# Bucketed attention ahead of two feed-forward layers on one core: value products in pairs from the start, other shares of the PSUM banks, partial sums exchanged by ScalarE

## The chip, the cores and the metric

The kernel runs on one core of a Trainium2 chip. The metric is the device time of one execution in microseconds (us); lower is better. Engines are named as in the profile: PE is TensorE's matmul stream and PEld its weight loads, DVE is VectorE, ACT is ScalarE, POOL is GpSimd, SP is SyncE, whose queue issues every DMA here (SPq in the rows).

## The reference, cut to what matters

```python
B, H, S, D = q.shape                                  # 2, 8, 768, 64
q_bits = (np.einsum('bhsd,dk->bhsk', q, proj) > 0)    # 6 bits a token, k alike
mask = q_bucket[:, :, :, None] == k_bucket[:, :, None, :]
scores = scale * np.matmul(q, k.transpose(0, 1, 3, 2))
scores = np.where(mask, scores, -1000000000.0)
scores = scores - np.max(scores, axis=-1, keepdims=True)
attn = np.exp(scores)
attn = attn / (np.sum(attn, axis=-1, keepdims=True) + 1e-09)
x = np.matmul(attn, v)                                # then 1536 tokens x 512
h = x @ w_in
x = (h * np.tanh(softplus(h))) @ w_out                # 512 -> 2048 -> 512
# then gate logits, 8 rounds of row and column scaling, and 8 experts,
# each relu(x @ w1[e]) @ w2[e], added with their weights
```

Attention has 16 heads of 768 tokens. The first feed-forward layer and the eight experts follow it on the same core. The change lies in attention, which takes about the first sixth of the time.

## The kernel before, in words

Attention works on half heads: 32 units `u`, each 384 queries of one head against its 768 keys. The heads 0 and 1 come first with both their halves (`u` 0 and 1 are head 0, `u` 2 and 3 head 1); after that two neighbouring heads alternate. Two half heads of equal half from two neighbouring heads make a pair `n` (`members`): pair 0 is `u` 0 and 2, pair 1 is `u` 1 and 3, pair 2 is `u` 4 and 5, and so on, 16 pairs. For a half head:

- `s_mm` makes the masked scores with queries on the partitions, in three tiles of 128 queries, each in one of two double banks of the ring `ps_r`; `s_max` (DVE) takes their row maximum; `rows_mm` (PE, `prow`) turns the maxima into a row, `rows_cp` (DVE) limits it, and a DMA carries it to the operand of the next step.
- `st_mm` makes the scores again, transposed: six chunks of 128 keys by 384 queries, two matmuls each (lines 408 and 409), in the two banks of `ps_t`; `st_exp` (ACT) writes their exponentials into one of `NP` = 14 tiles `p`, each with two tiny extra columns.
- `add` (POOL) sums three chunks of `p` into a tile `pa`, in two additions; there are two such tiles for a half head.
- the value product multiplies three chunks of `p` with `v` into a tile `pav` of 64 partitions for a half head. For the pairs 0 and 1, `av_one` does it for one half head at a time; from pair 2 on `av_mm` does it for both members, and a chunk's two matmuls go to different halves of TensorE's columns. `pav` has two banks, one for even and one for odd pairs (`ps_a`).
- `sum_mm` (`psum`, ring `ps_r`) sums the `pa` of a pair over the partitions: each member leaves two partial sums, in two groups of 32 partitions.
- `norm` ends a pair in parts: 0 transposes the sums (DVE, `rs`), 1 copies one column of 32 to `own` (ACT), four small DMAs (`norm_move`) bring the neighbouring group's copy to `other`, 3 adds the two and takes the reciprocal (DVE, `nr`), 4 transposes it back (DVE), 5 multiplies `pav` with it (DVE, `xu`), 6 and 7 split the result into a rounded tile `xh` (ACT) and the rest `xl` (POOL or DVE). Only part 5 makes the bank of `pav` free.

Queries and keys of a head are loaded into a landing tile `raw` (one, `NRAW` = 1, besides special places for the heads 1 and 2), split into a rounded part and a rest (`prep_hi`, `prep_lo`), moved by DMAs to the operands (`prep_move`, `bits_move`), and multiplied with the projection for the bucket bits (`bits_mm`, `pbits`; `bits_cmp`). In gaps of the engines the first weights of the layer that follows are loaded and decoded (`decode`, eight parts; part 6 is POOL's, part 7 an addition on DVE or POOL) and converted (`weight_hi` on ACT, `weight_lo` on POOL).

The order of all this on each engine is not written out: a small planner in the kernel lists the tasks with costs (`COST`), predecessors and due times, shifted by a table `OFF`, and emits the next task of the engine that is free first. Where it expects TensorE to be idle early on, it puts short filler matmuls (`keep_warm`, line 295, which write `warm`). Behind attention the first layer begins (`up`, lines 789 to 791, tile `h`); its fourth weight tile is converted only behind the last part of `norm`, since its memory was attention's.

Of the kernel before, what the change touches and what calls it, by code (L numbers as in the profile page):

```python
# [16 lines left out]
P = 128  # L17
# [21 lines left out]
NRAW = 1  # L39
NP = 14  # L40
NPA = 6
AVG = 3
AVD = 6
ENTER = 0.14
LEAVE = 0.2
ADDS = "P"
# [4 lines left out]
OFF = {'weight_lo': 16.9, 'add': -3.4, 'weight_load': -20.3, 'norm6': 66.2, 'prep_hi': -4.2, 'norm_move': -19.9, 'load_qk': 0.9, 'norm0': -16.1, 'load_v': -23.6, 'decode': 9.4, 'bits_mm': -6.9, 'norm1': -61.2, 'norm5': 11.9, 'st_exp': -7.0, 'norm7': 23.6, 'rows_cp': -10.6, 'av_mm': 0.7, 'rows_move': -20.0, 'rows_mm': 3.0, 'norm4': -35.4, 'norm3': 9.3, 'sum_mm': -0.6, 'bits_cmp': -14.6, 'av_one': 3.6, 'weight_hi': 63.6, 's_max': 0.0, 'st_mm': 2.1, 'prep_move': 6.5, 'prep_lo': -0.4, 'bits_move': -5.8, 's_mm': 2.4}  # L51
DELTA = 0.0524
# [3 lines left out]
PACE = 24  # L56
# [15 lines left out]
def lsh_attention_moe_kernel(  # L72
# [111 lines left out]
    def attention():  # L184
        with ExitStack() as a:
# [23 lines left out]
            xu = out_p.tile([P, 2, 512], F32, name="xu")  # L209
            rs = out_p.tile([P, S], F32, name="rs")  # L210
            nr = out_p.tile([P, HALF // 32], F32, name="nr")
            own, other = (out_p.tile([P, HALF // 32], F32, name=n) for n in ("own", "other"))
# [17 lines left out]
            def pair_of(u):  # L230
                return u % 2 if u < 4 else u // 2

# [42 lines left out]
            def clear_slots(j):  # L275
                for y in ps[j::2]:
                    nc.gpsimd.memset(y[:, HALF:WIDE], TINY)
# [6 lines left out]
            def warm_up():  # L284
                warm.append(slot(ps_t, "t", 0, 2, [P, 512], F32, "warm"))
                for _ in range(WARM):
                    nc.tensor.matmul(warm[0], xh[:, 0, 0:P], xh[:, 0, 0:512], start=True, stop=True)

            def keep_warm(n):
                if nm(av_one, 0, 0) in ends:  # L290
                    return
                if nm(st_mm, 0, 0) in ends and len(warm) == 1:
                    warm.append(slot(ps_a, "a", 0, 2, [P, 512], F32, "warm"))
                for _ in range(n):
                    nc.tensor.matmul(warm[-1][:, :FILL], xh[:, 0, 0:P], xh[:, 0, 0:FILL], start=True, stop=True)
# [47 lines left out]
            def bits_mm(h):  # L343
                psb_t[h] = next_r("pbits")[:, 0] if h else slot(ps_a, "a", 1, 2, [P, 512], F32, "pbits")
# [85 lines left out]
            def av_chunks(n, us, g):  # L430
                if n not in av_t:
                    av_t[n] = slot(ps_a, "a", n, 2, [P, 512], F32, "pav")
                for c in range(AVG * g, AVG * g + AVG):
                    for u in us:
# [5 lines left out]

            def av_one(u, g):
                av_chunks(pair_of(u), (u,), g)

            def av_mm(n, g):
                av_chunks(n, members(n), g)
# [42 lines left out]
            def task(engines, due, f, *args, after=(), cost=None, lag=0.01, ring=None, frees=None):  # L488
# [4 lines left out]
                "E": dict(warm_up=2.6, bits_mm=0.36, s_mm=0.355, rows_mm=0.06, st_mm=0.355, av_mm=0.66 * AVG, sum_mm=0.67, av_one=0.66 * AVG),  # L493
# [9 lines left out]
                    clear=0.6, prep_lo=1.0, add=1.03, norm=1.0, decode=1.3, weight_lo=1.27,  # L503
# [13 lines left out]
            def av_done(u, g):  # L517
                return nm(av_one, u, g) if u < 4 else nm(av_mm, pair_of(u), g)
# [10 lines left out]
            for j in range(2):  # L529
                task("P", -20 + j, clear_slots, j, cost=0.35)  # L530
# [41 lines left out]
            for u in range(NU):  # L572
# [14 lines left out]
                for c in range(NKC):  # L587
                    i = 6 * u + c
                    old = order[i - NP] if i >= NP else None
                    task("E", i - 4.0, st_mm, u, c, after=ready + [nm(st_exp, *order[i - 2])] * (i > 1))  # L590
# [7 lines left out]
            for n in range(NU // 2):  # L598
# [3 lines left out]
                room = [nm(norm, n - 2, 5)] if n > 1 else [nm(bits_cmp, 0, 1, 0)] * n  # L602
                for g in range(NKC // AVG):
                    for part in [(u,) for u in us] if n < 2 else [us]:
                        f, x = (av_one, part[0]) if n < 2 else (av_mm, n)
                        task("E", 6 * part[-1] + AVG * g + AVD, f, x, g,
                             after=[nm(st_exp, u, c) for u in part for c in range(AVG * g, AVG * g + AVG)] + ([nm(f, x, g - 1)] if g else room)
                             + [nm(load_v, head(u)) for u in part] + [nm(clear_slots, j) for j in range(2)] * (n < 2))
# [7 lines left out]
                task("D", due, norm, n, 3, cost=0.35, after=[nm(norm_move, n, x) for x in range(4)] + [nm(norm, n - 1, 4)] * (n > 0))  # L616
# [16 lines left out]
            for n in range(NCH):  # L633
# [5 lines left out]
                for part, (e, cost) in enumerate(costs):  # L639
# [4 lines left out]
                        7: [nm(decode, i, j, 6)] + ([nm(weight_lo, i - NDEC, 1)] if i >= NDEC else []),  # L644
# [32 lines left out]
            def groups(k):  # L677
                return int(tasks[k][3] in (bits_mm, rows_mm, av_one, av_mm, sum_mm))

            def begin(e, k):  # L680
# [8 lines left out]
                if e == "E":  # L689
                    real += (0.0, ENTER, LEAVE)[groups(k) - mode[0]]  # L690
# [14 lines left out]
            while count < len(tasks):  # L705
# [13 lines left out]
                if e == "E":  # L719
                    mode[0] = groups(k)  # L720
# [46 lines left out]
    nc.vector.memset(csum, 0.0)  # L767
# [230 lines left out]
    at(NST - 9, open_t)  # L998

# [326 lines left out]
```

## Time and profile before

| | us |
|---|---|
| runs of the kernel before, median of 3 | 1507.12 |
| their lowest and highest | 1504.7 and 1508.23 |
| the profiled execution's own time | 1506.02 |
| the span of its profile | 1504.2 |

The span is the time between the first and the last recorded instruction; 1.8 us of the profiled execution's time lie around it. The granted clock of TensorE was 1.00 throughout. A matmul's row is longer than the time that it holds up the next one, since matmuls are pipelined: what a matmul costs is read from its start to the start of the next.

### The profile page before, as it was taken

What the parts mean: (1) busy time and instruction counts of PE and PEld (TensorE: products, weight loads), DVE (VectorE), ACT (ScalarE), POOL (GpSimd) and SP (SyncE); (2) the same over time, 40 slices, a digit from 0 to 9 for tenths busy, and PEclk for the clock granted to TensorE, in tenths of its full rate; (3) what the DMA queues carried; (4) which work ended last, traced back from release to release, by engine and by line L of the source; (5) the groups of instructions that cost most, each with busy time, mean ns of one, the idle gap of its engine ahead of it and who ended that gap; (6) DMA issues with size and microseconds to landing.
All of it is one profiled execution on the core that took longest, in us unless ns stands there. A gap on an engine that the chain in (4) does not pass through costs nothing.

```text
span 1504.2 us, 20253 instructions
## 1 busy us (share of the span) xinstructions
PE 1487.8 (99%) x7448; PEld 1254.2 (83%) x7448; DVE 866.2 (58%) x1394; ACT 628.9 (42%) x1113; POOL 910.8 (61%) x756
## 2 busy tenths in 40 slices
PE   9999999999999999999999999999999999999998
PEld 5555556888887899989899998989989899998987
DVE  6888886877625566665445467653534535344353
ACT  4555555544334343334334333343433334333331
POOL 7787874433222776666666666666666666666660
PEclk9999999999999999999999999999999999999999
DMA  7666531222200122222122222232222212222211
GB/s 181 168 153 165 155 82 43 87 80 72 70 1 15 45 83 70 71 70 71 58 69 70 71 70 71 64 106 70 70 71 70 65 64 69 70 71 71 71 43 42
DMA packets 69563, 116.81 MB, mean 78 GB/s; under 512 B 21348, under 2 KB 23512, under 8 KB 69464
## 3 DMA queue, kind: packets, MB, share of 16 engines
q1 hardware_dynamic: 69464, 115.53, 25.8%
q8 instruction: 58, 0.95, 0.3%
q14 instruction: 41, 0.34, 0.1%
HBM read 93.41 MB, written 3.15 MB: 64 GB/s over the span
## 4 chain that ended last, share of the span: by engine, by line
PE 93%; DVE 2%; DMA 2%; SPq 1%; issue 1%; ACT 0%; POOL 0%; DVEq 0%; ACTq 0%
PE y L1178 35%; PE u L1111 31%; PE y L814 9%; PE pav L436 4%; PE h L791 3%; PE h L790 3%; PE h L789 3%; PE pst L408 2%; PE ps L373 2%; PE pst L409 1%; DMA raw<-in_qk_dram 1%; DVE mx L378 1%; PE psum L452 1%; SPq L329 1%; PE pbits L347 0%
## 5 line engine op out<-in xcount | busy, mean ns | idle before, releaser
L1119 ACT ACTIVATE gh<-c 128x384 fp32r<-128x384 f32 x256 | 134.6, 526 | 174.3 <-DVE c L1131 172.3
L1131 DVE TENSOR_TENSOR u<-u,p 128x384 f32<-128x384 f32 x64 | 35.7, 558 | 283.7 <-PE u L1111 283.7
L1124 DVE SCALAR_TENSOR_TENSOR gl<-c,gh 128x384 fp32r<-128x384 f32 x256 | 196.0, 828 | 0.0
L1178 PE MATMUL y<-ww,gh 128*128 128x512 f32 x768 | 186.6, 391 | 0.0
L1178 PE MATMUL y<-w,gh 128*128 128x512 f32 x768 | 186.0, 391 | 0.0
L1178 PEld LDWEIGHTS y<-w,gh 128*128 128x128 f32 x768 | 143.7, 188 | 28.9
L1178 PEld LDWEIGHTS y<-ww,gh 128*128 128x128 f32 x768 | 143.7, 188 | 28.8
L994 POOL TENSOR_TENSOR w<-stage,w 128x1024 fp32r<-128x1024 f32 x32 | 76.3, 2386 | 89.1 <-ACT w L990 89.1
L994 POOL TENSOR_TENSOR ww<-stage,ww 128x1024 fp32r<-128x1024 f32 x32 | 76.3, 2384 | 81.7 <-ACT ww L990 81.7
L414 ACT ACTIVATE p<-pst 128x384 f32<-128x384 f32 x192 | 88.4, 490 | 79.1 <-PE pst L409 73.0
L814 PE MATMUL y<-gh,w 128*128 128x512 f32 x336 | 109.7, 389 | 0.0
L158 POOL TENSOR_TENSOR stage<-stage,sgn 128x512 f32<-128x512 f32 x32 | 43.2, 1351 | 103.2 <-DVE sgn L156 93.1
L990 ACT CAST ww<-stage 128x1024 fp32r<-128x1024 f32 x32 | 33.6, 1052 | 157.5 <-PE y L1178 157.5
L970 POOL TENSOR_TENSOR wa<-stage,wa 128x512 fp32r<-128x512 f32 x32 | 45.6, 1424 | 89.0 <-ACT wa L965 80.0
L1178 PE MATMUL y<-ww,gl 128*128 128x512 f32 x384 | 98.2, 389 | 0.0
L990 ACT CAST w<-stage 128x1024 fp32r<-128x1024 f32 x32 | 33.6, 1050 | 154.5 <-PE y L1178 154.5
L1178 PE MATMUL y<-w,gl 128*128 128x512 f32 x384 | 97.7, 389 | 0.2 <-DVE gl L1124 0.2
L378 DVE TENSOR_REDUCE mx<-ps 128x1 f32<-128x768 f32 x96 | 88.4, 946 | 11.4 <-PE ps L373 10.9
L970 POOL TENSOR_TENSOR wx<-stage,wx 128x512 fp32r<-128x512 f32 x32 | 45.4, 1419 | 80.5 <-ACT wx L965 80.5
L1111 PE MATMUL u<-tw,w 128*128 128x384 f32 x480 | 91.7, 336 | 0.0
L1111 PE MATMUL u<-tw,ws 128*128 128x384 f32 x480 | 91.7, 336 | 0.0
L1178 PEld LDWEIGHTS y<-w,gl 128*128 128x128 f32 x384 | 72.0, 188 | 15.5 <-DVE gl L1124 0.6
(199 smaller groups left out, 3633.3 us busy)
## 6 DMA issues: line engine op xcount, KB each, us to landing
stage<-in_w_dram SPq DMA_DIRECT2D x160, 512.0 KB
raw<-in_qk_dram SPq DMA_DIRECT2D x13, 384.0 KB
sb<-hi SPq DMA_DIRECT2D x20, 192.0 KB
vt<-in_v_dram SPq DMA_DIRECT2D x16, 192.0 KB
out_dram<-acc SPq DMA_DIRECT2D x11, 256.0 KB
wx<-hi SPq DMA_DIRECT2D x14, 192.0 KB
zq<-hi SPq DMA_DIRECT2D x10, 192.0 KB
ak<-hi SPq DMA_DIRECT2D x10, 192.0 KB
```

Of the source, the lines that this page charges most:

```text
L378: nc.vector.tensor_reduce(out=mx_t[u % 2][:, t:t + 1], in_=s_t.pop((u, t))[:, :, :HALF], axis=AX.XY, op=ALU.max, negate=True)
L414: nc.scalar.activation(p_t[u, c][:, :HALF], st_t.pop((u, c))[:, :HALF], AF.Exp, scale=0.125)
L436: nc.tensor.matmul(av_t[n][64 * e:64 * e + 64, :WIDE], vt[head(u) // 2 % 2][:, c, e, :], p_t[u, c][:, :WIDE], start=(c == 0), stop=(c == N ...
L789: nc.tensor.matmul(t, wt[:, 0, f], xh[:, kc, c], start=(kc == 0), stop=False)
L814: nc.tensor.matmul(yps[j], x, y, start=(head and m == 0), stop=(tail and m == 2))
L970: nc.gpsimd.tensor_sub(a[:, 1, 0:512], t[:, 0, :], f32(a)[:, 0, 0:512])
L990: nc.scalar.copy(wbuf[u % 2]["w"][:, 0, :], staged["u", u, 1].rearrange("p c n -> p (c n)"))
L994: nc.gpsimd.tensor_sub(y[:, 1, :], t, f32(y)[:, 0, :])
L1111: nc.tensor.matmul(bank[x], weight(u, a, m, kc), moving(u, b, mm, kc), start=(first and n == 0), stop=(n == 5), skip_group_check=not first)
L1119: nc.scalar.activation(hi, src, AF.Relu)
L1124: nc.vector.scalar_tensor_tensor(out=lo, in0=src, scalar=0.0, in1=f32(hid_u[u, c][0]), op0=ALU.max, op1=ALU.subtract)
L1178: nc.tensor.matmul(y_t[t], (hi, hi, lo)[m][:, t % 3 * P:(t % 3 + 1) * P], y, start=(k == 0 and first), stop=(k == NF // 2 - 1 and last),)
```

## The change

All pairs use `av_mm`; `av_one` is gone. PSUM's eight banks are shared out anew: `ps_t` has three banks instead of two, `pav` one instead of two, so that a pair's first value product waits for part 5 of `norm` of the pair in front of it (`room`). The exchange of the partial sums is done by four ScalarE copies of 32 partitions each from `rs` into `other` in place of one copy and four DMAs. There are two landing tiles `raw`. `NP` is 13; the six chunks of `u` = 1 go into the decode tiles `dec`, which are not needed that early. The planner tells three kinds of TensorE task apart instead of two, some costs and the table `OFF` are others, and the memset of `csum` stands later.

```diff
-NRAW = 1
-NP = 14
+NRAW = 2
+NP = 13
+NT3 = 3
-AVD = 6
+AVD = 9
+TURN = 0.1
...
-DELTA = 0.0524
+DELTA = 0.0397
-PACE = 24
+PACE = 26
...
+            ps_t = a.enter_context(tc.tile_pool(name="ps_t", bufs=1, space=bass.MemoryType.PSUM))
             ps_r = a.enter_context(tc.tile_pool(name="ps_r", bufs=1, space=bass.MemoryType.PSUM))
-            ps_t = a.enter_context(tc.tile_pool(name="ps_t", bufs=1, space=bass.MemoryType.PSUM))
...
+            def place(u, c):
+                return NKC * (u - (u > 1)) + c
...
-                t = slot(ps_t, "t", NKC * u + c, 2, [P, 512], F32, "pst")
+                t = slot(ps_t, "t", NKC * u + c, NT3, [P, 512], F32, "pst")
...
-                p_t[u, c] = ps[(NKC * u + c) % NP]
+                p_t[u, c] = dec[c // 2][:, c % 2 * 512:c % 2 * 512 + 512] if u == 1 else ps[place(u, c) % NP]
...
-            def av_chunks(n, us, g):
+            def av_mm(n, g):
                 if n not in av_t:
-                    av_t[n] = slot(ps_a, "a", n, 2, [P, 512], F32, "pav")
+                    av_t[n] = slot(ps_a, "a", 0, 1, [P, 512], F32, "pav")
...
-            def norm_move(n, x):
-                y = x ^ 1
-                nc.sync.dma_start(out=other[32 * x:32 * x + 32], in_=own[32 * y:32 * y + 32])
...
-                    nc.scalar.copy(own, first)
+                    for y in range(4):
+                        nc.scalar.copy(other[32 * y:32 * y + 32], first[32 * (y ^ 1):32 * (y ^ 1) + 32])
                 elif part == 3:
-                    nc.vector.scalar_tensor_tensor(out=nr, in0=other, scalar=EPS, in1=own, op0=ALU.add, op1=ALU.add)
+                    nc.vector.scalar_tensor_tensor(out=nr, in0=other, scalar=EPS, in1=first, op0=ALU.add, op1=ALU.add)
...
-                room = [nm(norm, n - 2, 5)] if n > 1 else [nm(bits_cmp, 0, 1, 0)] * n
+                room = [nm(norm, n - 1, 5)] if n else []
...
-                task("A", due, norm, n, 1, cost=0.2, after=[nm(norm, n, 0)] + [nm(norm, n - 1, 3)] * (n > 0))
-                for x in range(4):
-                    task("Q", due, norm_move, n, x, lag=0.3, after=[nm(norm, n, 1)])
+                task("A", due, norm, n, 1, cost=0.85, after=[nm(norm, n, 0)] + [nm(norm, n - 1, 3)] * (n > 0))
...
-    nc.vector.memset(csum, 0.0)
+    at(NST // 2, nc.vector.memset, csum, 0.0)
```

What this does to the order is seen at three places. The first is TensorE's first value product, a good 20 us into the program; `prow` is the row of maxima, `ps` the scores for the maxima, `pst` the transposed scores, and the numbers behind names tell buffers apart. Before:

```order
L387 MATMUL prow<-idt,mx_153 1x128 x3
L436 MATMUL pav<-p_133,vt_124 64x386
L436 MATMUL pav<-p_134,vt_124 64x386
L436 MATMUL pav<-p_135,vt_124 64x386
L373 MATMUL ps<-sb_115 128x384 x2
L408 MATMUL pst<-zq_118,ak_121 128x384
L409 MATMUL pst<-sb_115 128x384
L373 MATMUL ps<-sb_116 128x384 x2
```

Now:

```order
L414 MATMUL pst<-sb_115 128x384
L441 MATMUL pav<-p_132,vt_124 64x386
L441 MATMUL pav<-p_138,vt_124 64x386
L441 MATMUL pav<-p_133,vt_124 64x386
L441 MATMUL pav<-p_139,vt_124 64x386
L441 MATMUL pav<-p_134,vt_124 64x386
L441 MATMUL pav<-p_140,vt_124 64x386
L394 MATMUL prow<-idt,mx_151 3x128
L451 MATMUL psum<-pa_145,ones 32x384
```

Three products of half head 0 stood there alone, behind 12 transposed chunks; now six of two half heads stand together, two by two, behind 21 chunks. Over all of attention the value products before come in 8 groups for one half head and 28 for a pair, now in 32 for a pair, and TensorE goes over from scores to the other kinds of matmul 41 times instead of 37.

The second place is DVE's order in the steady part, from the reciprocal of one pair to its `xu`. Before:

```order
L469 SCALAR_TENSOR_TENSOR nr<-other,own 128x12
L470 RECIPROCAL nr<-nr 128x12
L472 STREAM_TRANSPOSE rs<-nr 128x384
L378 TENSOR_REDUCE mx_153<-ps 128x1 x3
L465 STREAM_TRANSPOSE rs<-psum 128x384
L350 TENSOR_SCALAR bit<-pbits,cst 128x192
L477 SCALAR_TENSOR_TENSOR xu<-pav,rs 128x384
```

Now, from the transposed sums to `xu` of the same pair:

```order
L460 STREAM_TRANSPOSE rs<-psum 128x384
L162 TENSOR_TENSOR dec_83<-stage 128x512
L405 TENSOR_SCALAR row<-prow 3x128
L465 SCALAR_TENSOR_TENSOR nr<-other,rs 128x12
L466 RECIPROCAL nr<-nr 128x12
L468 STREAM_TRANSPOSE rs<-nr 128x384
L383 TENSOR_REDUCE mx_152<-ps 128x1 x2
L473 SCALAR_TENSOR_TENSOR xu<-pav,rs 128x384
```

Before, `xu` of a pair could stand behind the transposed sums of the next one; now the whole chain of a pair stands together, with two row maxima in front of `xu`.

The third place is DVE's order at the end of attention, behind the last `psum`. Now:

```order
L460 STREAM_TRANSPOSE rs<-psum 128x384
L162 TENSOR_TENSOR dec_85<-stage 128x512
L465 SCALAR_TENSOR_TENSOR nr<-other,rs 128x12
L466 RECIPROCAL nr<-nr 128x12
L468 STREAM_TRANSPOSE rs<-nr 128x384
L473 SCALAR_TENSOR_TENSOR xu<-pav,rs 128x384
L162 TENSOR_TENSOR dec_85<-stage 128x512
L422 CAST xh<-xu 128x384
L425 TENSOR_TENSOR xl<-xu,xh 128x384
```

Both halves of the fourth weight tile's last decode step (`dec_85`) have moved into this stretch; before, both were done ahead of it, one on DVE and one on POOL.

## Rows read from the trace of the kernel before

**Rows 1.** By stretch: us; PE, PEld, DVE, ACT, POOL busy (instructions); clock, DMA, GB/s.

```profile
0.00:13.60 13.60, 11.24 (x60) 7.62 (x61) 10.62 (x23) 9.16 (x12) 10.03 (x31) 1.00 0.69 184
13.60:58.40 44.80, 44.67 (x217) 26.42 (x215) 32.20 (x47) 21.17 (x45) 29.89 (x31) 1.00 0.71 175
58.40:222.00 163.60, 157.38 (x934) 94.06 (x933) 138.12 (x218) 90.66 (x196) 131.46 (x124) 1.00 0.56 141
222.00:247.00 25.00, 21.61 (x111) 12.88 (x110) 12.71 (x22) 9.69 (x21) 14.22 (x12) 1.00 0.14 43
```

**Rows 2.** PE's timeline: value products of one half head, and of a pair.

```profile
22.43 2.16 PE L436 MATMUL pav<-p,vt 128*64 128x386 f32 x6
...
152.25 2.17 PE L436 MATMUL pav<-p,vt 128*64 128x386 f32 x12
```

**Rows 3.** PE's timeline: a chunk of transposed scores on time, and one late.

```profile
154.81 0.34 PE L408 MATMUL pst<-zq,ak 128*128 128x384 f32 x1
154.99 0.34 PE L409 MATMUL pst<-sb 97*128 97x384 f32 x1
...
155.61 0.44 PE L408 MATMUL pst<-zq,ak 128*128 128x384 f32 x1
155.89 0.34 PE L409 MATMUL pst<-sb 97*128 97x384 f32 x1
```

**Rows 4.** Line 408 with its weight loads: what ended its idle time (us, times).

```profile
  ACT p L414: 13.8, 51
```

**Rows 5.** DVE's groups of 0 to 247 us: busy, mean ns, idle before.

```profile
L378 DVE TENSOR_REDUCE mx<-ps 128x1 f32<-128x768 f32 x96 | 88.4, 946 | 11.4 <-PE ps L373 10.9
...
L477 DVE SCALAR_TENSOR_TENSOR xu<-pav,rs 128x384 f32<-128x384 f32 x16 | 9.7, 607 | 0.1
L465 DVE STREAM_TRANSPOSE rs<-psum 128x384 f32<-128x384 f32 x16 | 9.3, 579 | 9.1 <-PE psum L452 9.1
...
L400 DVE TENSOR_SCALAR row<-prow 3x128 fp32r<-3x128 f32 x28 | 7.6, 273 | 10.2 <-PE prow L389 10.0
```

**Rows 6.** PE's waits: us in total, times, longest.

```profile
PE pbits L347 <- DMA raw<-in_qk_dram: 3.3, 4, 1.4
```

**Rows 7.** Timeline: a pair's first value product, and the pair before's xu.

```profile
40.71 2.16 PE L436 MATMUL pav<-p,vt 128*64 128x386 f32 x6
...
53.79 0.61 DVE L477 SCALAR_TENSOR_TENSOR xu<-pav,rs 128x384 f32<-128x384 f32 x1
...
208.07 2.17 PE L436 MATMUL pav<-p,vt 128*64 128x386 f32 x12
...
209.84 0.60 DVE L477 SCALAR_TENSOR_TENSOR xu<-pav,rs 128x384 f32<-128x384 f32 x1
```

**Rows 8.** Timeline of the end of attention, engines apart, put in order.

```profile
233.65 1.30 POOL L158 TENSOR_TENSOR stage<-stage,sgn 128x512 f32<-128x512 f32 x1
234.87 0.85 PE L452 MATMUL psum<-pa,ones 128*32 128x384 f32 x8
235.86 0.58 DVE L465 STREAM_TRANSPOSE rs<-psum 128x384 f32<-128x384 f32 x1 [2.66 <-PE psum L452]
236.50 0.50 PE L789 MATMUL h<-xh,w 128*128 128x512 f32 x1 [0.78 <-DVE rs L465]
236.52 0.21 ACT L467 COPY own<-rs 128x12 f32<-128x12 f32 x1 [2.77 <-DVE rs L465]
236.76 2.40 SPq L456 DMA_DIRECT2D other<-own  x4
240.55 0.17 DVE L469 SCALAR_TENSOR_TENSOR nr<-other,own 128x12 f32<-128x12 f32 x1 [3.67 <-DMA other<-own]
...
243.48 1.05 ACT L172 CAST w<-dec 128x1024 fp32r<-128x1024 f32 x1 [6.75 <-DVE csum L767]
244.61 2.36 POOL L178 TENSOR_TENSOR w<-dec,w 128x1024 fp32r<-128x1024 f32 x1 [8.55 <-ACT w L172]
...
247.02 0.50 PE L791 MATMUL h<-xh,w 128*128 128x512 f32 x1 [1.59 <-POOL w L178]
```

More of the change, by code (lines that the diff above doesn't have):

```diff
@@ L208, in attention @@
             vt = [sets.tile([P, NKC, 2, D], F32, name=f"vt{i}") for i in range(2)]
-            xu = out_p.tile([P, 2, 512], F32, name="xu")
+            xu = out_p.tile([P, 2, HALF], F32, name="xu")
             rs = out_p.tile([P, S], F32, name="rs")
             nr = out_p.tile([P, HALF // 32], F32, name="nr")
-            own, other = (out_p.tile([P, HALF // 32], F32, name=n) for n in ("own", "other"))
+            other = out_p.tile([P, HALF // 32], F32, name="other")
             pj = out_p.tile([P, 12], F32, name="pj")
@@ L275, in clear_slots @@
             def clear_slots(j):
-                for y in ps[j::2]:
+                for y in ps[j::2] if j < 2 else [x[:, k:k + 512] for x in dec[:3] for k in (0, 512)]:
                     nc.gpsimd.memset(y[:, HALF:WIDE], TINY)
@@ L502, in attention @@
                 "P": dict(
-                    clear=0.6, prep_lo=1.0, add=1.03, norm=1.0, decode=1.3, weight_lo=1.27,
+                    clear=0.6, prep_lo=1.0, add=1.05, norm=1.0, decode=1.3, weight_lo=1.27,
                 ),
@@ L528, in attention @@
             task("D", -8, proj_parts, after=[nm(clear_start), nm(load_const, 0)])
-            for j in range(2):
+            for j in range(3):
                 task("P", -20 + j, clear_slots, j, cost=0.35)
@@ L588, in attention @@
                     i = 6 * u + c
-                    old = order[i - NP] if i >= NP else None
-                    task("E", i - 4.0, st_mm, u, c, after=ready + [nm(st_exp, *order[i - 2])] * (i > 1))
+                    j = place(u, c) - NP
+                    old = order[j + (NKC if j >= NKC else 0)] if u != 1 and j >= 0 else None
+                    task("E", i - 4.0, st_mm, u, c, after=ready + ([nm(st_exp, *order[i - NT3])] if i >= NT3 else []) + [nm(bits_cmp, 0, 1, 0)] * (i == 2))
                     read = [av_done(old[0], old[1] // AVG), nm(add, old[0], old[1] // 3, max(old[1] % 3 - 1, 0))] if old else []
@@ L601, in attention @@
                 due = 6 * us[1]
-                room = [nm(norm, n - 2, 5)] if n > 1 else [nm(bits_cmp, 0, 1, 0)] * n
+                room = [nm(norm, n - 1, 5)] if n else []
                 for g in range(NKC // AVG):
[L604 to L608, printed above, removed]
+                    task("E", due + AVG * g + AVD, av_mm, n, g,
+                         after=[nm(st_exp, u, c) for u in us for c in range(AVG * g, AVG * g + AVG)] + ([nm(av_mm, n, g - 1)] if g else room)
+                         + [nm(load_v, head(u)) for u in us] + [nm(clear_slots, j) for j in range(3)] * (n < 2))
                 task("E", due + 8, sum_mm, n, after=[nm(add, u, g, 1) for u in us for g in range(2)] + [nm(norm, n - 2, 5)] * (n > 1), ring="r", frees=nm(norm, n, 0))
@@ L612, in attention @@
                 task("D", due, norm, n, 0, cost=0.58, after=[nm(sum_mm, n)] + ([nm(norm, n - 2, 5)] if n > 1 else raw))
[L613 to L616 removed]
+                task("A", due, norm, n, 1, cost=0.85, after=[nm(norm, n, 0)] + [nm(norm, n - 1, 3)] * (n > 0))
+                task("D", due, norm, n, 3, cost=0.45, after=[nm(norm, n, 1)] + [nm(norm, n - 1, 4)] * (n > 0))
                 task("D", due, norm, n, 4, cost=0.58, after=[nm(norm, n, 3)])
@@ L643, in attention @@
                         4: [nm(decode, i, j, 3)], 5: [nm(decode, i, j, 4)], 6: [nm(decode, i, j, 1), nm(decode, i, j, 5)],
-                        7: [nm(decode, i, j, 6)] + ([nm(weight_lo, i - NDEC, 1)] if i >= NDEC else []),
+                        7: [nm(decode, i, j, 6)] + ([nm(weight_lo, i - NDEC, 1)] if i >= NDEC else []) + ([av_done(1, x) for x in range(NKC // AVG)] + [nm(add, 1, g, x) for g in range(2) for x in range(2)] if i < 3 else []),
                     }[part]
@@ L675, in attention, with change @@
             mode = [0]
-            def groups(k):
-                return int(tasks[k][3] in (bits_mm, rows_mm, av_one, av_mm, sum_mm))
+            KIND = {av_mm: 1, sum_mm: 2, bits_mm: 2, rows_mm: 2}
+            def change(k):
+                a, b = mode[0], KIND.get(tasks[k][3], 0)
+                return 0.0 if a == b else LEAVE if not b else ENTER if not a else TURN
             def begin(e, k):
@@ L689, in begin @@
                 if e == "E":
-                    real += (0.0, ENTER, LEAVE)[groups(k) - mode[0]]
+                    real += change(k) if r - free[e] < 0.02 else max(0.1, change(k))
                 if e == "D" and shares(k):
@@ L719, in attention @@
                 if e == "E":
-                    mode[0] = groups(k)
+                    mode[0] = KIND.get(f, 0)
                 if e == "E" and nm(warm_up) in ends:
```

20 lines of the change are left out of this document (8 added, 12 removed).

## The prediction

> **What bounds the kernel now.** I read the stretches first [rows 1]. Attention ends at 247 us; everything behind it, 1257 us, is untouched but for one memset of 128x32. So the change is worth what it saves before 247 us, if TensorE sets the pace there. It seems to: PE is busy 44.67 of 44.80 us from 13.6 to 58.4, and 157.38 of 163.60 up to 222 (58.4 is where pair 2's first value product stands). But a PE row is longer than the time for which it holds up the next one, so this hides short waits, and I looked at who waits for whom. DVE, the next busiest with 138.12 of 163.60 us, waits for TensorE: 10.9 us for `ps`, 9.1 for `psum`, 10.0 for `prow`, 30.0 us together [rows 5]. TensorE's own long waits are few: 3.3 us for the landing of queries and keys [rows 6], and 0.78 and 1.59 us at the end [rows 8]. So TensorE is the bound, with DVE not far behind (84% of the steady stretch), and what shortens its stream shortens the kernel, until DVE or a new wait takes over.
>
> **The change, part by part.** The sum starts from the profiled execution's own 1506.0 us; the median of the runs shown is 1.1 us above it.
>
> *Pairs from the start.* Three chunks of one half head take TensorE 2.16 us, and three chunks of two half heads 2.17 [rows 2]: a pair costs what one member costs. Eight single groups go (8 x 2.16 = 17.3), four pair groups come (4 x 2.17 = 8.7): 8.6 us less. It counts in full if TensorE has other work meanwhile. The bounds are 0 and -8.6. Against the full gain: DVE is busy 42.8 of the first 58.4 us [rows 1], and would have to fit into some 50, at 86%; and the planner puts nine more filler matmuls there, which stand where it expects TensorE to wait. I put 1.5 us of the 8.6 back.
>
> *The third bank for transposed scores.* A chunk on time has its second matmul 0.18 us behind the first; one that had to wait for `st_exp` starts late and has it 0.28 us behind, since the stream was broken [rows 3]. Line 408 with its weight loads was let go by `st_exp` 51 times, after 13.8 us of idle time in all [rows 4]; much of that is a weight load that waits while the matmul in front still streams. Bounds: 0 and -13.8. The least that 51 breaks cost is 51 x 0.10 = 5.1 us, and the late starts come on top; I take -6.5. ScalarE is not the next limit: it is busy 90.66 of 163.60 us [rows 1], and its copies for the exchange add 64 x 0.21 - 16 x 0.21 = 10 us over all of attention [rows 8].
>
> *The second landing tile.* It can remove the 3.3 us for which `pbits` waited for `raw` [rows 6]. Those loads are also issued behind other DMAs on one queue, and that queue loses its 64 exchange DMAs, 2.40 us for every four [rows 8], some 38 us of issuing. Bounds 0 and -3.3; I take -2.5.
>
> *The end of attention.* From the last transposed sums to `nr` it takes 240.55 - 235.86 = 4.69 us [rows 8]. With ScalarE's copies it is 0.58 for the transposition, at most 4 x 0.21 for the copies, and some 0.2 for two handovers: 1.6, so 3.1 less. The next row, ScalarE's weight conversion at 243.48, then gets a new predecessor on DVE between `xu` and `xh`: the last half of a decode step. No row has it at this place; its cost lies between 0 and the 1.05 us of the conversion, which has twice the columns and the same partitions, and I take 1.0. It needs POOL's part of that half, which now stands behind two weight conversions; POOL was free of additions at 233.65, 1.2 us before `psum` began, and has about 5 us until `xu`, for two decode parts of 1.30 and the two halves of a conversion that takes 2.36 as a whole (together 5.0): just in time. So the matmul that waits until 247.02 can go 2.1 us earlier. From `psum` at 234.87 to there TensorE has 12.15 - 0.78 - 1.59 = 9.8 us of work, so up to 2.4 are to be had; the 0.78 goes since the first `h` tiles now lie in the banks of the transposed scores, not of `psum`. I take -2.0; bounds 0 and -2.4.
>
> *More changes of kind.* TensorE leaves the scores 41 times instead of 37. Each visit breaks the stream on the way in and on the way out, at 0.10 each by the late chunk [rows 3]: 4 x 0.2 = +0.8. Bounds 0 and +1.5.
>
> *One bank for the value products.* This is the new wait. A pair's first product must now stand behind `xu` of the pair in front. Before, it never did: at all 15 handovers it began before that `xu` ended, by 209.84 + 0.60 - 208.07 = 2.4 us at least and 53.79 + 0.61 - 40.71 = 13.7 at most [rows 7]. Queued behind it on TensorE is everything: scores, maxima and the next exponentials. What is there instead is a shorter chain. From the start of `psum` the sums are transposed 1.0 us later (234.87 to 235.86) for 0.58 [rows 8]; copies and handovers take 1.0; `nr`, its reciprocal and the transposition back about 1.1 (0.17, a reciprocal of the same small tile, 0.58, and gaps); that makes 3.7. But in DVE's order two row maxima of 0.95 [rows 5] stand in front of `xu`, and they wait for `ps` tiles that TensorE makes only after the pair's second value product. Counted along TensorE's new order: `psum` 0.8, value product 2.17, a row of maxima, then chunks at 0.35 (twice 0.18) and `ps` tiles at the same price; the second `ps` ends near 4.9, its maximum near 5.9, `xu` near 6.6. TensorE itself reaches the next first product after 0.8 + 2.17 + 10 x 0.35 + 0.2 = 6.7. So chain and stream meet within 0.1 us, and any delay on DVE becomes TensorE's. I take 0.27 us for each of 15 handovers, +4. Bounds: 0, and the 15 x 2.4 = +36 that the old lateness would cost.
>
> *At nothing:* the 13th instead of a 14th `p` tile, the use of `dec` and the later memset. The first two could make ScalarE wait, which has 45% of its time free [rows 1]; without that cover a late exponential costs what the two-bank wait cost, 0.10 and its lateness.
>
> Sum: -8.6 + 1.5 - 6.5 - 2.5 - 2.0 + 0.8 + 4.0 = -13.3, so 1492.7. I say **1493 us**, by its own between 1487 and 1498.
>
> [...]
>
> **The rivals.**
>
> *The single value bank decides (slower).* Its place is the handover; DVE is in order, and one late `ps`, `lo` or decode step ahead of `xu` delays it. The point from which it decides: the sum without the +4 is -17.3, so at 17.3 / 15 = 1.15 us of waiting per handover nothing is left. With 1.5 us it is 1506.0 - 17.3 + 22.5 = 1511. For it: before, `xu` was 2.4 us late at best. Against it: that lateness came with the exchange by DMA, 4 us between `own` and `nr` [rows 8], and with an order in which `xu` might wait.
>
> *The gain is taken back (little changes).* If TensorE early on waits for DVE and the moves instead (the pairing gives 2 instead of 7.1) and DVE, at 84%, lets only half of the bank's 6.5 through, the sum is -2 - 3.2 - 2.5 - 2.0 + 0.8 + 4 = -5: 1501. With a handover of 0.5 us more it is no change, 1505 to 1508. For it: DVE's and POOL's work is the same in less time. Against it: DVE waited 30 us for TensorE [rows 5].
>
> *The third bank gives all.* All of the 13.8 and 3.3, and a handover that costs nothing: -8.6 + 1.5 - 13.8 - 3.3 - 2.4 + 0.8 = -25.8: 1480. For it: DVE would still be no more than 88% busy (193.7 us of its work in the four stretches, in 221 us). Against it: some of the 13.8 is covered already.
>
> **How the numbers follow.** Chances: my forecast (1487 to 1498) 0.50; the gain partly taken back (1498 to 1504) 0.18; more than forecast (under 1487) 0.15; no change 0.07; slower 0.10. 0.2% (3 us) is about what a measurement can tell from no change; the first three cases lie beyond it: faster 0.83, same 0.07, slower 0.10. The range leaves out the lower part of the good case and the cases of no gain: 1483 to 1503.
>
> **What the profile would show.** Right: all value products as rows of 12 at 2.17 us, the first near 28 us, pair 2's near 49 instead of 58; the idle time of the transposed scores' line put down to `st_exp` under 5 us; no `raw` wait of `pbits`; the first layer's late matmul near 234 instead of 247. Wrong: first value products of a pair with idle time put down to `xu`, over 1 us each; early `prow` or `ps` rows waiting for DVE; the late matmul near 247 or behind it.

## The result, and the profile after

The changed kernel takes **1490.12 us** (median of 4 runs, 1489.08 to 1490.93) against 1506.25 before (median of 4, 1504.7 to 1508.23): a ratio of 0.9892, 95% interval 0.9875 to 0.9909. The profiled execution took 1490.93 us with a span of 1489.1, which is 15.1 less than before. The forecast was 1493, in 1483 to 1503.

The stretches of the changed kernel, cut where those of [rows 1] are cut (the first value product of pair 2 stands at 48.60, the first of the last pair at 218.08), and two short stretches that come up at the end; columns as there:

```profile
0.00:13.60 13.60, 11.90 (x55) 8.24 (x56) 10.58 (x22) 9.15 (x12) 10.19 (x36) 1.00 0.74 198
13.60:48.60 35.00, 34.71 (x216) 24.18 (x215) 27.36 (x45) 21.24 (x50) 26.82 (x29) 1.00 0.87 207
48.60:218.08 169.48, 163.20 (x989) 104.41 (x988) 148.33 (x227) 104.18 (x248) 140.24 (x131) 0.99 0.52 138
...
59.00:60.70 1.70, 0.40 (x3) 0.08 (x1) 0.61 (x2) 1.51 (x6) 1.46 (x2) 1.00 0.88 228
...
62.30:65.70 3.40, 3.40 (x11) 3.33 (x11) 3.33 (x6) 2.28 (x5) 1.95 (x3) 0.52 0.75 274
```

By stretch it came near the forecast, if the term of the pairs is laid to the first stretch, that of the end to the last and the others between:

| stretch | before | after | difference | forecast |
|---|---|---|---|---|
| start to pair 2's first value product | 58.43 | 48.60 | -9.8 | -7.1 |
| from there to the last pair's first | 172.4 | 169.5 | -2.9 | -4.2 |
| from there to the late matmul of the first layer | 16.2 | 14.1 | -2.1 | -2.0 |

The sum, -14.8, is nearly the whole of the 15.1. Of the signs by which the prediction was to be right, five came: all value products stand in rows of 12, the first near 28 (28.34), pair 2's near 49, the late matmul near 234 (232.22), and the wait of `pbits` for `raw` [rows 6] is gone. One was missed: the idle time put to `st_exp` is 6.2 us, not under 5. TensorE's waits (us in total, times, longest) up to 235 us:

```profile
PE prow L394 <- DVE mx L383: 1.7, 2, 0.8
...
PE pst L413 <- ACT p L419: 1.5, 2, 1.0
PE ps L378 <- DMA sb<-hi: 1.3, 1, 1.3
...
PE pav L441 <- DVE xu L473: 0.2, 1, 0.2
```

The value bank shows 0.2 us. The idle time of the transposed scores' first line with its weight loads, 51 times and 13.8 us in [rows 4], is now:

```profile
  ACT p L419: 6.2, 12
```

DVE's groups up to 235 us (busy, mean ns, idle before) answer to [rows 5]. It waits for TensorE 6.8, 4.7 and 7.5 us, 19.0 together where it was 30.0:

```profile
L383 DVE TENSOR_REDUCE mx<-ps 128x1 f32<-128x768 f32 x96 | 88.3, 948 | 7.9 <-PE ps L378 6.8
...
L460 DVE STREAM_TRANSPOSE rs<-psum 128x384 f32<-128x384 f32 x16 | 9.2, 577 | 4.7 <-PE psum L451 4.7
...
L405 DVE TENSOR_SCALAR row<-prow 3x128 fp32r<-3x128 f32 x28 | 7.5, 269 | 8.2 <-PE prow L394 7.5 <-PE psum L451 0.4
L465 DVE SCALAR_TENSOR_TENSOR nr<-other,rs 128x12 f32<-128x12 f32 x16 | 7.1, 447 | 1.6 <-ACT other L463 1.4
```

From the timeline: a short handover, a long one, and the end of attention.

```profile
36.18 0.62 DVE L473 SCALAR_TENSOR_TENSOR xu<-pav,rs 128x384 f32<-128x384 f32 x1
...
36.85 0.54 PE L441 MATMUL pav<-dec,vt 128*64 128x386 f32 x1 [0.24 <-DVE xu L473]
...
204.38 0.60 DVE L473 SCALAR_TENSOR_TENSOR xu<-pav,rs 128x384 f32<-128x384 f32 x1
...
206.88 2.17 PE L441 MATMUL pav<-p,vt 128*64 128x386 f32 x12
...
222.12 0.85 PE L451 MATMUL psum<-pa,ones 128*32 128x384 f32 x8
...
223.12 0.58 DVE L460 STREAM_TRANSPOSE rs<-psum 128x384 f32<-128x384 f32 x1 [0.83 <-PE psum L451]
...
223.41 2.99 POOL L180 TENSOR_TENSOR wx<-dec,wx 128x512 fp32r<-128x512 f32 x2
...
223.79 0.91 ACT L463 COPY other<-rs 32x12 f32<-32x12 f32 x4 [4.52 <-DVE rs L460]
...
225.18 1.27 DVE L465 SCALAR_TENSOR_TENSOR nr<-other,rs 128x12 f32<-128x12 f32 x1
...
232.22 0.50 PE L786 MATMUL h<-xh,w 128*128 128x512 f32 x1 [0.40 <-POOL w L180]
```

The first handover leaves 36.85 - 36.80 = 0.05 us, the other 206.88 - 204.98 = 1.90. Of the 15, seven leave 0.05 to 0.61 us and eight 1.9 to 4.2. From `psum` to the late matmul it is 10.1 us, 12.15 in [rows 8].

### The profile page after: what moved, and what is told of

Same layout as the page of the kernel before. It is cut to its first block, busy times and chain, and to the rows that moved or that the text cites. A ratio compares the mean times of both kernels' runs of the same rounds, so it can differ in the third digit from the quotient of the medians.

```text
span 1489.1 us, 20182 instructions
## 1 busy us (share of the span) xinstructions
PE 1476.4 (99%) x7457; PEld 1258.9 (85%) x7457; DVE 871.2 (59%) x1393; ACT 638.3 (43%) x1161; POOL 913.9 (61%) x762
## 4 chain that ended last, share of the span: by engine, by line
PE 96%; DVE 2%; issue 1%; ACT 1%; DMA 1%; POOL 0%; DVEq 0%; ACTq 0%; SPq 0%; POOLq 0%
PE y L1174 35%; PE u L1107 32%; PE y L809 9%; PE pav L441 4%; PE h L786 3%; PE h L784 3%; PE h L785 3%; PE pst L413 2%; PE ps L378 2%; PE pst L414 2%; PE psum L451 1%; DVE mx L383 1%; PE pbits L352 0%; PE lg L837 0%; PE prow L394 0%
## 5 line engine op out<-in xcount | busy, mean ns | idle before, releaser
L419 ACT ACTIVATE p<-pst 128x384 f32<-128x384 f32 x186 | 82.6, 490 | 46.8 <-PE pst L414 33.3
```

## The experiments

In each the computation is the reference's. "Order kept" means that every engine's instructions stand in the changed kernel's order; otherwise the planner makes its order anew from the same table of numbers (in e5 and e12 from that of before), and the time then holds the edit and the new order together.

### The banks: e1, e2 and e10

e1 gives the transposed scores two banks and leaves one idle; e2 gives that one to the value products; e10 has e1's order, instruction for instruction, but three banks for the scores.

```diff
-NT3 = 3
+NT3 = 2
```

The same and, for e2:

```diff
-                    av_t[n] = slot(ps_a, "a", 0, 1, [P, 512], F32, "pav")
+                    av_t[n] = slot(ps_a, "a", n, 2, [P, 512], F32, "pav")
...
-                room = [nm(norm, n - 1, 5)] if n else []
+                room = [nm(norm, n - 2, 5)] if n > 1 else [nm(bits_cmp, 0, 1, 0)] * n
```

For e10, with NT3 at 3:

```diff
-                    task("E", i - 4.0, st_mm, u, c, after=ready + ([nm(st_exp, *order[i - NT3])] if i >= NT3 else []) + [nm(bits_cmp, 0, 1, 0)] * (i == 2))
+                    task("E", i - 4.0, st_mm, u, c, after=ready + [nm(st_exp, *order[i - 2])] * (i > 1) + [nm(bits_cmp, 0, 1, 0)] * (i == 2))
```

> The changed kernel with two banks for the transposed scores again and still one for the value products; the bank set free lies idle, and the planner makes its order anew. All work is the same. The forecast's term for the third bank says +6.5 us against the changed kernel's 1490.1, so 1496 to 1497, and the line of the transposed scores waiting for the exponential again some 50 times for 13.8 us (changed: 12 times, 6.2 us). The rival reads the changed kernel's steady stretch, which is only 2.9 us shorter than before with the third bank, the landing tile and the single value bank together: the late starts were mostly covered, so +2 to +3, 1492 to 1493. If the bank is worth nothing, 1490 +- 1.

> As the kernel with two score banks, but the idle bank goes back to the value products, which then have two, and a pair's first product waits only for the normalisation two pairs back. Its time less that of the kernel with two score banks is the price of the single value bank. The forecast's term says 4 us less (0.27 us at each of 15 handovers). The rival counts the handovers of the changed kernel's trace: only five have under 0.2 us to spare and the wait put down to them is 0.2 us in all, so the price is under 1 us and the two kernels agree. The first rival of the prediction (1.5 us per handover) would make it 22 us less.

> The order of the kernel with two score banks (1503.1 us), instruction for instruction on every engine, but with three banks given to the transposed scores. Only the number of banks differs between the two, so the difference is what the third bank is worth in a fixed order; what is left to the changed kernel's 1490.1 us is the order. The forecast's term says 6.5 us less, 1496 to 1497, and the rest, some 6.5, is the order. If the bank is worth what its undoing cost (13 us), 1490. By the waits for the exponential that the profile puts down (4.6 us against 1.5) it is 3 us, 1500.

Measured: e1 1503.06 us (ratio to before 0.9986, 0.9977 to 0.9995), e2 1504.89 (0.9995, 0.9986 to 1.0004), e10 1500.05 (0.9956, 0.9944 to 0.9969). So in one and the same order the third bank is worth 3.0 us by the medians and 4.5 by the ratios; runs of the two at an equal granted clock differ by 2.6 us (0.998) and 3.1 (0.999). 9.9 us more lie between two orders of the same resources, e10 and the changed kernel. With the second value bank e2 gains nothing that shows, but its order is another than e1's, so it gives no price for that bank in a fixed order. The idle time of the scores' first line with its weight loads, put to `st_exp`, in e1 and then in e10:

```profile
  ACT p L419: 21.4, 49
```

```profile
  ACT p L419: 8.0, 17
```

32 waits and 13.4 us of idle time less, for 3.0 us. Counted at the matmuls, their own waits for `st_exp`, without those of weight loads, fall from 4.6 us to 1.3; and the chunks whose second matmul starts over 0.22 us behind the first fall from 83 to 62, which at the 0.10 us of [rows 3] is 2.1 us. Together that is more than 3.0, so what the 3.0 us are made of stays open.

### The value bank's slack: e7 and e8

The transposition back, 0.58 us on DVE, is done twice for each pair, order kept: in e7 ahead of `xu`, in e8 behind it.

```diff
                 elif part == 5:
+                    nc.vector.transpose(
+                        out=rs[:, c].rearrange("p (b j) -> p b j", j=32),
+                        in_=nr.unsqueeze(2).to_broadcast([P, HALF // 32, 32]),
+                    )
                     nc.vector.scalar_tensor_tensor(
```

In e8 the same lines stand behind the multiplication.

> The changed kernel in its own order with one more VectorE instruction for each pair, ahead of the product that sets the value bank free: the transposition of 0.58 us done twice. The result is the same. The forecast's account (chain and stream meet within 0.1 us at each handover) says that 15 x 0.58 = 8.7 us come on top of what the load on VectorE costs (the kernel with the same instruction behind the product tells that). By the margins of the changed kernel's trace only the handovers under 0.58 us lose, by 0.53 + 0.50 + 0.51 + 0.12 + 0.43 = 2.1 us.

> The control: the changed kernel in its own order with the same additional transposition of 0.58 us for each pair, put directly behind the product that sets the value bank free. The result is the same. Theory of a bound TensorE: VectorE has 12% of the steady stretch free, so 16 x 0.58 = 9.3 us of additional work on it cost little, 0 to +3 us. If VectorE is by now the co-bound (it waits for TensorE only some 19 us in all), a good part of the 9.3 us shows, +4 or more.

Measured: e7 1495.70 us (0.9931, 0.9918 to 0.9943), e8 1493.60 (0.9916, 0.9902 to 0.9929). Ahead of `xu` it costs 2.1 us more than behind it (the runs, 1494.49 to 1496.72 and 1492.20 to 1494.21, do not overlap). That is what the five handovers give that have less than 0.58 us to spare, 0.53 + 0.50 + 0.51 + 0.12 + 0.43 = 2.1; if all 15 were as tight as the prediction has it, it would be 8.7. The first of them in e7, where `xu` is 0.72 us later and the product 0.73:

```profile
36.90 0.62 DVE L477 SCALAR_TENSOR_TENSOR xu<-pav,rs 128x384 f32<-128x384 f32 x1
...
37.58 0.54 PE L441 MATMUL pav<-dec,vt 128*64 128x386 f32 x1 [0.85 <-DVE xu L477]
```

The control is no zero: 16 x 0.58 = 9.3 us of work on DVE, off this path, cost 3.5 us. So DVE is nearly a second bound.

### The exchange: e4, e6 and e11

One copy and four DMAs in place of ScalarE's four copies: in e4 for all pairs, with the planner told; in e11 for all pairs, order kept; in e6 for the last pair alone, order kept.

```diff
-                    for y in range(4):
-                        nc.scalar.copy(other[32 * y:32 * y + 32], first[32 * (y ^ 1):32 * (y ^ 1) + 32])
+                    nc.scalar.copy(own, first)
+                    for x in range(4):
+                        norm_move(n, x)
```

This is e11. In e6 it holds for the last pair, and in e4 the four moves are tasks of the queue, as before the change.

> The changed kernel with the exchange of the partial sums by one copy and four transfers for all pairs, as before the change; the planner knows their costs and makes its order anew. The single value bank stays. The forecast's account of the handover (chain and stream meet within 0.1 us) says that a chain 3.1 us longer is laid bare at 15 handovers, unless the order moves: up to +45. By the margins in the changed kernel's trace (five to seven handovers under 0.6 us to spare, eight near 2.2 or more) it is 5 x 3 + 2 x 2.5 + 8 x 0.9 = +27. The rival: the planner puts the next value product later and fills TensorE with scores, so only the end costs, +2 to +3: 1493. This tells whether the copies on ScalarE are what makes one value bank possible.

> The changed kernel in its own order, except that the last pair alone exchanges its partial sums by one copy and four transfers. The forecast's term for the end says +2.0 us (the 3.1 us that the exchange saves, less what the decode step put between the product and its rounding hides), 1492. The rival: TensorE's late matmul there waits for the weight conversion on ScalarE and GpSimd, not for the normalisation, or has other work until then, so 0 to +0.5. It could also come out at +3.1, if the whole exchange lies on the path.

> The changed kernel in its own order, with the exchange of the partial sums by one copy and four transfers for all pairs. The instructions of TensorE, VectorE and GpSimd stand in the same order. The value product then becomes free some 3.1 us later at each handover, which the order cannot avoid. The forecast's account (chain and stream meet) says 15 x 3.1 = +46; the margins of the changed kernel's trace say 7 x 2.8 + 8 x 0.9 = +27, and 3.2 of the end (the kernel whose last exchange alone was undone): 1517 to 1520. If TensorE waits, its granted clock falls to half in stretches, as it did after a wait in the changed kernel's trace: each of 3.4 us would add some 1.5 us. The rival: the transfers hold up other transfers of the queue, not the value bank, and the waits are for queries and keys: the same size, but no waits put down to the product that frees the bank.

Measured: e4 1526.29 us (1.0143, 1.0113 to 1.0174), e6 1493.32 (0.9920, 0.9906 to 0.9933), e11 1561.69 (1.0370, 1.0356 to 1.0385). The last exchange is worth 3.2 us; in e6 the late matmul waits for the conversions that follow `nr`:

```profile
222.06 0.21 ACT L467 COPY own<-rs 128x12 f32<-128x12 f32 x1 [4.47 <-DVE rs L464]
...
222.30 2.49 SPq L455 DMA_DIRECT2D other<-own  x4
...
227.93 0.18 DVE L473 SCALAR_TENSOR_TENSOR nr<-other,rs 128x12 f32<-128x12 f32 x1 [4.35 <-DMA other<-own]
...
233.93 0.50 PE L794 MATMUL h<-xh,w 128*128 128x512 f32 x1 [1.71 <-POOL w L180]
```

All exchanges together are worth far more than the handovers: e11 loses 71.6 us, where the account of the prediction gave 46 and the margins 27 to 30. What ended the idle time of DVE's line `nr` in e11, TensorE's longest waits there, and one case from the timelines of DVE and PE:

```profile
  DMA other<-own: 58.5, 15
```

```profile
PE ps L378 <- DVE row L405: 23.0, 8, 6.1
PE ps L378 <- DVE mx L383: 13.0, 5, 4.8
PE pav L441 <- DVE xu L478: 10.1, 2, 6.3
```

```profile
100.37 0.28 DVE L405 TENSOR_SCALAR row<-prow 3x128 fp32r<-3x128 f32 x1 [0.77 <-PE prow L394]
105.71 0.17 DVE L470 SCALAR_TENSOR_TENSOR nr<-other,own 128x12 f32<-128x12 f32 x1 [5.06 <-DMA other<-own]
...
107.66 1.01 PE L378 MATMUL ps<-sb 96*128 96x384 f32 x2 [4.77 <-DVE mx L383]
```

DVE stands at `nr` for 5 us, the row maxima (`mx`) behind it wait, and TensorE stops at `ps`, since its bank is not read yet. At other pairs the limited row (`row`) stands there instead. In all, TensorE stops 36.0 us at `ps` and 10.1 at `pav`. The account and the margins had put the wait at the value bank, and the rival at queries and keys; most of it came at what is queued behind `nr` on DVE. Up to 33 of the 71.6 us are the lower clock, 0.979 over the profile (below). In e4 the planner makes an order in which `nr` idles for the transfers only 9.1 us, and still loses 36 us: the value bank is TensorE's longest wait there, 7.1 us, and up to 18 us are the lower clock, 0.988.

### The landing tile: e3

```diff
-NRAW = 2
+NRAW = 1
```

> The changed kernel with one landing tile for queries and keys. All work is the same. The forecast's term says +2.5 us (0 to 3.3), 1492.6, with a wait of the bucket bits for the landing tile in TensorE's waits again (3.3 us before, none in the changed kernel). The rival: the wait went because the queue lost its 64 exchange transfers, not because of the tile; then no such wait, and 1490 +- 1.

Measured: 1496.32 us (0.9944, 0.9932 to 0.9957), 6.2 more, and no wait of `pbits` for `raw` comes back. So it has the size of neither theory. The loss lies between pair 3, which begins 5.1 us earlier than in the changed kernel (61.84 against 66.93), and pair 8, which begins 7.6 later (138.58 against 131.02), in another order. Between them, from 92.66 to 109.85, the granted clock is 0.80, which is up to 17.19 x 0.20 = 3.4 us of the 6.2. What the tile would do in one order was not separated.

### The pairs, and the planner's numbers: e5, e12 and e13

e5 is the kernel before with pairs from the start and nothing else. e12 is the changed kernel with the planner's numbers of before. e13 is the changed kernel, order kept, but in pairs 0 and 1 one member's three chunks go ahead of the other's.

```diff
-                p_t[u, c] = ps[(NKC * u + c) % NP]
+                p_t[u, c] = dec[c // 2][:, c % 2 * 512:c % 2 * 512 + 512] if u == 1 else ps[place(u, c) % NP]
...
-                    for part in [(u,) for u in us] if n < 2 else [us]:
-                        f, x = (av_one, part[0]) if n < 2 else (av_mm, n)
+                    for part in [us]:
+                        f, x = av_mm, n
```

These are the main lines of e5. For e12 (the table `OFF` is before's too):

```diff
-AVD = 9
+AVD = 6
...
-DELTA = 0.0397
+DELTA = 0.0524
...
-PACE = 26
+PACE = 24
```

And for e13:

```diff
-                for c in range(AVG * g, AVG * g + AVG):
-                    for u in members(n):
+                work = [(u, c) for c in range(AVG * g, AVG * g + AVG) for u in members(n)]
+                for u, c in sorted(work) if n < 2 else work:
```

> The kernel before with one part of the change alone: value products in pairs from the start, with the chunks of the second half head in the decode tiles. Banks, landing tile, exchange and the planner's numbers stay as before. The forecast says 7.1 us less (8.6 with nothing put back) than before's 1506.2: 1498 to 1499. The changed kernel's trace has pair 2's first value product 9.8 us earlier, for all edits together. The rival: the early part waits for VectorE and the moves instead, and the pairing gives some 2 us: 1504.

> The changed kernel with all its edits, except that the planner's due times and their shifts (the table, its slope, the start of the value products and the pace of the loads) are those of before. All work is the same; only the order differs. If the gain is one of resources, as every term of the forecast has it, it is 1490 to 1494. If the numbers that set the order carry a good part of it, 1500 or more; the kernel before with pairs alone, whose numbers were not fitted to pairs, took 1524.

> The changed kernel in its own order, except that in the value products of pairs 0 and 1 the three chunks of one half head go ahead of the three of the other, as before the change, instead of alternating. 4 groups of 2.17 us become 4 of 4.32. The forecast's term for the pairs says +8.6, less 1.5 that TensorE would have waited anyway: +7.1, 1497. The rival, that the early part waits for VectorE and the moves whatever TensorE does, says +2 or less: 1492.

Measured: e5 1523.98 us (1.0122, 1.0105 to 1.0140), e12 1520.89 (1.0098, 1.0084 to 1.0111), e13 1490.81 (0.9900, 0.9885 to 0.9915). With before's numbers all the edits of memory and instructions together are 15.0 us slower than before; the numbers turn that into 15.8 less, by these medians 30.8 us, of which up to 15 are the lower clock of e12, 0.990 over the profile (below). Pairs alone, in the order made for them, bring pair 2's first product from 58.43 to 57.45 only, and lose 18 us in all. e12's windows from the first to the second pair's first product, and of its steady stretch, and one wait from its timeline:

```profile
26.80:45.00 18.20, 15.29 (x85) 9.72 (x84) 10.15 (x17) 6.09 (x16) 8.15 (x9) 0.85 0.85 215
...
56.40:247.03 190.63, 174.92 (x977) 104.66 (x976) 155.24 (x235) 102.22 (x244) 140.41 (x128) 0.94 0.52 126
```

```profile
40.08 1.62 PE L378 MATMUL ps<-sb 96*128 96x384 f32 x4 [2.01 <-DVE mx L383]
```

In the first, TensorE is busy 84% of the time and DVE 56%, where each waits for the other in turn, and the granted clock is 0.85.

e13 does not do what was expected of it: the twelve matmuls of a group last not 4.32 but 30.69 - 27.89 = 2.80 us, to the start of what follows, against 30.44 - 28.34 = 2.10 when they alternate. Its timeline:

```profile
27.89 2.86 PE L441 MATMUL pav<-p,vt 128*64 128x386 f32 x12
```

So it adds 4 x 0.7 = 2.8 us to TensorE, not 8.6. Pair 2's first product comes 2.3 us later, counted from the first of all; the medians differ by 0.7 us, and the intervals overlap. It says that some of TensorE's time there is free, and nothing firm of the 8.6.

## Why the time was right, and which steps were not

The total came as forecast and the three stretches near it, but the split by edit did not, and one large part had no term. In the middle stretch two errors cancel, a third bank counted some 3 us too high and a value bank counted too dear by up to 4: that it came near is in part luck.

- **The order had no term.** "The change part by part" priced memory, instructions and waits in an order taken as given, and gave the planner's numbers nothing. e12 shows that they carry 30.8 us, more than the whole gain: without them the edits lose. The sum leaned on the new order where its steps were read off it (the handover's count, the decode step at the end), and the edits are not worth their terms by themselves. Whether before's resources with the new numbers would gain was not tried.
- **Pairs, -7.1 with 1.5 put back.** The stretch up to pair 2 gave -9.8 with all edits and the new order, so the put-back was not needed there. But e5 gives -1.0 there for the pairs under before's numbers: whether TensorE has other work meanwhile, which the term supposed, then depends on the order. In the changed kernel's own order the 2.8 us that e13 adds to TensorE there show as 0.7.
- **Third bank, -6.5.** Mis-sized: 3.0 in one order, that of e1. The 0.10 us of a break holds: over the 83 late chunks of e1 the median is 0.28 us, over the others 0.18. But the 51 waits that were multiplied by it are those of the weight loads, and 12 of them stayed. 51 - 12 = 39 at 0.10 make 3.9, and nothing on top of that is seen in the 3.0.
- **Landing tile, -2.5.** The wait that it was to remove is gone, but it stays away with one tile too (e3), and with two tiles it stays away when the 64 transfers are back (e4, e11). With one tile and the transfers it is there, 3.3 us before and 3.5 in e5. So in these orders either of the two causes that the prediction names removes it, and the tile is not needed for that.
- **The end, -2.0.** Right: -2.1 in the rows, and 3.2 for the exchange alone (e6), where 3.1 was worked out. It was had although `nr` took 1.27 us in place of 0.17.
- **One value bank, +4.** Too dear. It was counted as if all handovers had the pattern of one, where chain and stream meet within 0.1 us. Eight of them have 1.9 us or more to spare, the profile puts 0.2 us to it, and 0.58 us more in front of `xu` cost 2.1 us, not 8.7 (e7 against e8). So the overlap of `xu` with the next pair's products, which the second value bank allowed, was hardly missed here, with the short exchange.
- **The first rival** (the bank decides) was put aside since before's lateness came with the exchange by DMA. e4 and e11 bear that out and go further: with the DMAs back the kernel is 36 or 72 us slower, in e11 mostly by what waits behind `nr`. The prediction priced the exchange at the end, and in the steady stretch only as transfers that leave the queue.
- **DVE as the next bound.** Near: 9.3 us more on it cost 3.5 (e8).
- **Changes of kind, +0.8, and what was put at nothing** (the 13th tile, `dec`, the memset): no run changes one of these alone.
- Where the steady stretch gave 1.3 us less than forecast, the profiled run shows one wait of 1.3 us for a transfer (`sb`) and, behind it, 3.4 us at a clock of 0.52 (below). That this is the cause is not shown: the other runs, two of them at 1490.12 us, have a clock of 1.00.

## What to carry to other kernels

When a change brings a scheduler's tuned numbers along, give the order a term of its own, and test each edit in a fixed order: here the same edit measured 3 us in one order and 13 with a new one, and all of them together lost 15 us under the old numbers. Price a missing buffer by what it delays in the matmul stream, and best by a run in a fixed order (3.0 us here), not by the idle time of its weight loads (13.4 us). For an instruction that waits, look first at what stands behind it in its engine's order: in e11 the waits of `nr` for the exchange, 5.06 us in the case shown, stopped TensorE through the row maxima and the limited rows (36 us) more than through the bank that `nr` was to free (10).

## What the runs showed of the hardware that was not expected

**The clock fell behind a wait of 1.3 us.** In the changed kernel's profile TensorE is busy 0.40 of 1.70 us from 59.00 on, waiting for a transfer; from 62.30 to 65.70, busy throughout, its granted clock is 0.52. A matmul of the transposed scores lasts 0.52 us there and holds up the next one for 0.32, against 0.34 and 0.18 just ahead of it. 3.40 x 0.48 = 1.6 us are lost there, behind a wait of 1.3. Not every such wait is followed by a fall: before the change TensorE waited up to 1.4 us for `raw` [rows 6] and 1.59 at the end [rows 8], and the clock was 1.00 throughout. Four kernels with more waits have a lower clock. TensorE's listed waits up to 260 us (270 in e12 and e11) are 20.0 us in e5, 20.8 in e12, 29.5 in e4 and 46.3 in e11, against 8.4 in the changed kernel and 11.6 before. The clock is 0.94 over e12's steady stretch, which is 190.63 x 0.06 = 11 us of full clock, of the 21 us by which that stretch is longer than the changed kernel's. Over the whole profile it is 0.994 in e5, 0.990 in e12, 0.988 in e4 and 0.979 in e11, which is up to 9, 15, 18 and 33 us of full clock, each time about half of what the kernel loses (e5 against the kernel before, the others against the changed one). No term of the forecast had this half. No run shows what makes the clock fall behind one wait and not behind another.

**Members in turn overlapped.** In e13 all six matmuls of one half head (the profile has two rows for each of its three chunks) stand ahead of the six of the other in the program. In pair 1 the chunks of the first of the two lie in `dec`, so that its rows are told from the other's:

```profile
37.32 1.19 PE L441 MATMUL pav<-dec,vt 128*64 128x386 f32 x3
38.03 0.54 PE L441 MATMUL pav<-p,vt 128*64 128x386 f32 x1
38.34 0.49 PE L441 MATMUL pav<-dec,vt 128*64 128x386 f32 x1
38.40 0.49 PE L441 MATMUL pav<-p,vt 128*64 128x386 f32 x1
38.67 0.49 PE L441 MATMUL pav<-dec,vt 128*64 128x386 f32 x1
38.73 0.49 PE L441 MATMUL pav<-p,vt 128*64 128x386 f32 x1
38.99 0.49 PE L441 MATMUL pav<-dec,vt 128*64 128x386 f32 x1
39.05 1.14 PE L441 MATMUL pav<-p,vt 128*64 128x386 f32 x3
40.12 0.27 PE L394 MATMUL prow<-idt,mx 128*3 128x128 f32 x1
```

The second half head's first matmul starts at 38.03, ahead of three of the first's. From there two rows of starts run side by side, each at 0.32 to 0.37 us, until the first half head has had its last at 38.99 and the other goes on alone. The rows from 43.05 on have the same pattern. All four such groups of e13 take 2.79 or 2.80 us to the start of what follows, where two separate groups take 2 x 2.16 [rows 2].

**One small DVE instruction took 0.17 to 1.27 us.** `nr`, 128x12, takes 0.17 us in [rows 8] and 1.27 at the end of the changed kernel, where it ends at 226.45, while GpSimd's two conversions, 2.99 us together, end at 226.40. The 16 of them average 447 ns, and before the change 471, where the prediction's chain counted 0.17 for each. One more case, from the steady stretch:

```profile
177.55 1.54 POOL L160 TENSOR_TENSOR stage<-stage,sgn 128x512 f32<-128x512 f32 x1 [1.25 <-DVE sgn L158]
178.19 0.94 DVE L465 SCALAR_TENSOR_TENSOR nr<-other,rs 128x12 f32<-128x12 f32 x1 [0.25 <-ACT other L463]
```

GpSimd's row ends at 179.09, `nr` at 179.13. In the changed kernel six of the 16 take over 0.2 us, and each ends 0.03 to 0.05 us behind the GpSimd row that ran when it began; the ten others take 0.17 to 0.19. In e6 GpSimd is idle at the last one, and it takes 0.18. No run here moved the one against the other on purpose, so why they end together is not shown.
